# A linear-attention and MLP kernel: the last chunk's attention with keys by halves of a block, and the last two stores on another queue

## The chip, the core and the metric

The kernel runs on one core of a Trainium2 chip. The core has five engines that run side by side, each through its own list of instructions: TensorE (PE in the profile; its weight loads are listed apart as PEld), VectorE (DVE), ScalarE (ACT), GpSimd (POOL) and SyncE (SP). An instruction waits until the semaphores that it names have reached their values, and everything behind it on its engine waits with it. SP, ACT and POOL can also start DMA transfers; the profile calls the issuing lists SPq, ACTq and POOLq.

The metric is the device time of one execution in microseconds (us). The kernel before took 207.64 us as the median of three runs (207.38 to 207.97).

## The reference

Inputs are q, k, v of shape (4, 8, 768, 64) in fp32 (batch, heads, tokens, head size), one decay `lam` per head, and the two matrices and the slopes of an MLP. Attention is causal and decays with distance; it is computed in blocks with a running state. Its output, laid out as 3072 tokens by 512 features, goes through the MLP.

```python
intra = np.einsum('bhic,bhjc->bhij', qb, kb) * Dmask[None]      # Dmask = lam**(i-j) where i >= j, else 0
intra = np.einsum('bhij,bhjd->bhid', intra, vb)
inter = np.einsum('bhid,bhde->bhie', qb * lam_pow[None], kv_state)
out[:, :, sl] = intra + inter
kv_state = lam_block * kv_state + np.einsum('bhsd,bhse->bhde', kb * rev_pow[None], vb)
...
h = x @ w_in
g = np.maximum(h, 0.0) + alpha * np.minimum(h, 0.0)
return g @ w_out
```

The reference uses blocks of 64 tokens; the kernel uses blocks of `L` = 128, which is the same sum cut in another place.

## The kernel before, in words

**Chunks and units.** The 3072 tokens are cut in six chunks `c` = 0 to 5 (`NC` = 6) of 512 tokens: two of the four sequences times a window of 256 tokens (two blocks of 128, called a = 0 and 1 below). A chunk's attention is four *units* (`units`, numbered 0 to 23): one sequence and four of its heads each. Units 20 to 23 are the last chunk, `c` = 5.

**Layout.** Loads put tokens 2p and 2p+1 on partition p, so that a partition holds an even and an odd token (`e` = 0, 1). Each run that a load of k, q or raw v copies is 128 fp32 numbers, 512 bytes. `load` starts loads of k and q on SP (some early ones on POOL), `load_v16` starts those of v on POOL, one per unit, which cast to fp16 on the way; a unit's v is a tile of its own, from eight buffers.

**One unit.** `casts` turns k and q to fp16 (on ACT, for units 19 on) and multiplies k by its decay on POOL (`key_decayed`, L291, tile `kdec`). `transposes` (called through `turned`) has SP start a DMA transpose that gives `qkT`. `decayed` (L355, POOL) multiplies the transposed q by its decay, giving `qdT`. Then `cluster(old, new)` puts these on PE in a row: `inter(old)` (L375), `score_products(new)` (L391), `intra(old)` (L416), `state_products(new)` (L436). `score_products` and `intra` are 16 matmuls each: 64 by 64 corners of the array, four of them (the list `QUADS`) side by side in the array, each streaming 128 query columns. Half of the 128 keys of a block (the even or the odd ones) meet all its 128 queries in one matmul. `masked` (L402, DVE) multiplies the 1024 score columns by the decay mask (tile `dmask`, one fp32 value per score), which also sets the scores above the diagonal to zero. `attended` (ACT, L250) takes the sum to the tile `xT`, and `states` updates the running state on DVE (L465, tile `R`).

**The MLP.** `up` (L545) computes 128 rows of h on PE into a PSUM tile `h_ps`; ACT takes the negative part (L553, tile `m`), DVE finishes g (L560). `down` (L573), and for chunks 3 to 5 `down2` and `down2_last` (L655), multiply g by the second matrix. The latter use a scheme of seven instead of eight half products: sums of the halves of w_out are made on DVE (`weight_sum`, L621, tile `w_sum`) and sums of the halves of g on POOL and DVE (`g_sum`, L638).

**Order.** The order is written by hand and is the program order on every engine. Chunks 0 to 2 are a long list of calls. From chunk 3 on, a loop over `order[c]` alternates `up` of chunk c and `down` of chunk c-1 (each 0.86 us of PE), and the table `plan[c]` names what is called in front of the x-th of them. In chunk 3 the loop calls the loads of k and q for units 20 to 23 (x = 0 and 13), the preparation of units 19 to 23, and `cluster(16, 17)` to `cluster(19, 20)`; in chunk 4 `cluster(20, 21)` to `cluster(23, None)`. Chunk 5 has the MLP alone, and behind it stands `down2_last(5)`.

**The end.** `down2_last` finishes one output tile after the other. The last is computed as two times 128 columns (tile `p4`, written `p` in the profile): eight matmuls, an add on DVE (L719), a store by `write`, twice. All stores are started by SP. After them SP waits for the transfers that are still under way, and the engines meet at a barrier.

**DMA semaphores.** SP's transfers take eight semaphores in turn. A transfer waits, at its issue, until the one eight places before it has landed.

Of the kernel before, what the change touches and what calls it, by code (L numbers as in the profile page):

```python
# [11 lines left out]
def kernel(  # L12
# [33 lines left out]
    CH = 2 * W  # L46

# [3 lines left out]
    kv_pool = ctx.enter_context(tc.tile_pool(name="kvh", bufs=8))  # L51
    qkt_pool = ctx.enter_context(tc.tile_pool(name="qkt", bufs=3))
# [27 lines left out]
    def load(c, bi, x, half=None, queue="S"):  # L80
# [7 lines left out]
        i = "kqv".index(x)  # L88
        (nc.gpsimd if queue == "G" else nc.sync).dma_start(
# [130 lines left out]

    llp = const.tile([128, NHP], fp32, name="llp")
# [41 lines left out]
    def cast(n, name, eng):  # L263
        t = T.setdefault(n, {})
        if name == "v16":
            t[name] = kv_pool.tile([128, 4, 2, D], fp16, tag=name, name=name)
# [6 lines left out]

    def load_v16(n):

        c, bi, hh = units[n]
        v16 = kv_pool.tile([128, 4, 2, D], fp16, tag="v16", name="v16")
# [9 lines left out]
    def key_decayed(n, eng="G"):  # L287
        hh = units[n][2]
        kr = raw_of(n)["k16"]
        kdec = kv_pool.tile([128, 2, 4, D], fp16, tag="kdec", name="kdec")  # L290
# [3 lines left out]
            in1=kdecay[:, ds(4 * hh, 4), :].rearrange("p h e -> p e h").unsqueeze(3).to_broadcast([128, 2, 4, D]),  # L294
# [104 lines left out]
    def masked(n):  # L399
        t = T[n]  # L400
        t["sm"] = sm_pool.tile([128, 2, 2, 2, L], fp16, tag="sm", name="sm")
        nc.vector.tensor_tensor(  # L402
# [6 lines left out]
    def intra(n):  # L409
        t = T[n]  # L410
        pb = units[n][0] // 2
        for hp in range(2):
            for e in range(2):
                for hl, a in QUADS:
                    p = ds(a * 64, 64)
                    nc.tensor.matmul(  # L416
                        ot[a][ds(hl * 64, 64), hp, :],
                        lhsT=t["v16"][p, 2 * hp + hl, e, :],
                        rhs=t["sm"][p, hl, hp, 1 - e, :],
# [244 lines left out]
    def write(c, e, half, o, b=None, of=ds(0, 256)):  # L664
# [3 lines left out]
        if b is None:  # L668
            nc.sync.dma_start(out=to, in_=o)
        else:  # L670
            nc.sync.dma_start(out=to[:, b, of], in_=o)
# [34 lines left out]
    def down2_last(c):  # L706
# [3 lines left out]
        for i, side, b in order:  # L710
# [3 lines left out]
            if (i, b) == (4, 1):  # L714
                for x, bank in enumerate(("s", "acc")):
# [4 lines left out]
                    write(c, 1, 0, o, b, ds(128 * x, 128))  # L720
# [208 lines left out]
    query_decay(3, 0)  # L929
    up(1, 2, None, "h")  # L930
# [39 lines left out]
    down(1, 3, 0, 4, "op")  # L970
    down(1, 0, 2, 4, "tk")
# [67 lines left out]
    def prepared(n):  # L1039
        casts(n, "AA")  # L1040

    def turned(n):
        transposes(n, "D", False)
# [9 lines left out]
            13: lambda: (turned(20), decayed(19), load(5, 1, "k"), load(5, 1, "q")),  # L1053
            17: lambda: prepared(21),
            18: lambda: cluster(18, 19),
            20: lambda: (turned(21), decayed(20)),
            24: lambda: prepared(22),
# [78 lines left out]
```

## Time and profile before

| what | value |
|---|---|
| median of three runs | 207.64 us |
| the profiled execution's own time | 207.89 us |
| its span, first to last instruction | 206.1 us |
| PE busy | 200.1 us, 97% of the span |
| DVE, ACT, POOL busy | 77%, 55%, 54% |
| granted PE clock | 0.996 of full |
| the stage from 104 to 134 us | chunk 3's loop: `up` of chunk 3, `down` of chunk 2, units 16 to 20 |
| the stage from 134 to 162 us | chunk 4's loop as far as unit 23 |
| the stage from 162 us on | the MLP alone |

In the profile a group's row gives source line, engine, operation, tiles and shapes, the count, then busy time in us and the mean time of one in ns, then how long the engine stood idle in front of these and what it waited for. In a timeline, rows begin with the start and the length of a merged run of instructions, in us. Matmuls overlap, so the distance between starts is what one costs when the engine is full, not its own length.

### The profile page before, as it was taken

Reading aid. Unit: us, or ns where it says so; the run is one execution under the profiler, and the core shown is the slowest. Engines: PE = TensorE matmul, PEld = TensorE weight load, DVE = VectorE, ACT = ScalarE, POOL = GpSimd, SP = SyncE. Lnnn points to the kernel's source line nnn. Section 1 sums busy time; section 2 is a strip of 40 time slices with the busy share of each in tenths; the row PEclk is TensorE's granted clock in tenths of the full one; section 3 lists DMA queues with packets and bytes.
Section 4 is the critical chain, followed back from the end, with each engine's and each line's share of the span. In section 5 each row is a group of like instructions: output and inputs, shape, how many; then the busy total and the mean of one; then the engine's idle time right before and its main releaser. Section 6 shows DMA issues by size and latency. Waiting matters only on the chain.

```text
span 206.1 us, 5587 instructions
## 1 busy us (share of the span) xinstructions
PE 200.1 (97%) x2271; PEld 122.8 (60%) x2271; DVE 159.1 (77%) x289; ACT 113.6 (55%) x210; POOL 110.3 (54%) x132
## 2 busy tenths in 40 slices
PE   7999999999999999999999999999999999999991
PEld 6976445556445465555555455467667666667881
DVE  6978889568889647899998897959999466675921
ACT  7885778144776218656767466643543644444220
POOL 8999794043468893196356995562094040642000
PEclk9999999999999999999999999999999999999998
DMA  6999999997999998999969974441001201012222
GB/s 164 277 197 234 244 260 206 234 287 231 225 230 257 203 237 189 245 158 125 188 108 276 213 176 88 64 102 42 12 0 54 90 15 51 2 54 71 83 77 79
DMA packets 58206, 31.18 MB, mean 151 GB/s; under 512 B 27124, under 2 KB 55940, under 8 KB 58180
## 3 DMA queue, kind: packets, MB, share of 16 engines
q1 hardware_dynamic: 43028, 21.25, 42.5%
q0 software_dynamic: 15136, 9.57, 29.3%
q8 instruction: 18, 0.29, 0.6%
q14 instruction: 8, 0.07, 0.1%
q10 hardware_dynamic: 16, 0.00, 0.0%
HBM read 27.27 MB, written 6.29 MB: 163 GB/s over the span
## 4 chain that ended last, share of the span: by engine, by line
PE 92%; DVE 2%; ACT 2%; issue 1%; ACTq 0%; DVEq 0%
PE h_ps L545 39%; PE o_ps L573 21%; PE o_ps L655 16%; PE s L391 4%; PE acc L416 3%; PE unread L152 3%; PE acc L375 2%; PE tpx L341 2%; PE acc L436 1%; DVE g L638 1%; ACT L180 1%; ACT m L553 1%; ACT xT L250 1%; DVE sm L402 1%; PE p L655 0%
## 5 line engine op out<-in xcount | busy, mean ns | idle before, releaser
L545 PE MATMUL h_ps<-xT,w_in_sb 128*128 128x512 f16 (+1 forms) x392 | 91.9, 375 | 0.2 <-DVE g L560 0.2
L560 DVE SCALAR_TENSOR_TENSOR g<-m,oma,h_ps 128x512 f16<-128x512 f32 (+1 forms) x98 | 71.1, 734 | 24.9 <-ACT m L553 21.7
L553 ACT ACTIVATE m<-h_ps 128x512 f32<-128x512 f32 (+1 forms) x98 | 57.3, 588 | 46.3 <-PE h_ps L545 40.3
L545 PEld LDWEIGHTS <-w_in_sb 128*128 128x128 f16 x392 | 37.6, 98 | 37.4 <-issue 0.4
L573 PE MATMUL o_ps<-w_out_sb,g 128*128 128x512 f16 x192 | 46.8, 380 | 0.0
L402 DVE TENSOR_TENSOR sm<-s,dmask 128x1024 f16<-128x1024 f32 x24 | 29.2, 1219 | 11.7 <-PE s L391 11.7
L655 PEld LDWEIGHTS <-g 128*128 128x128 f16 x296 | 28.2, 98 | 8.2
L638 POOL TENSOR_TENSOR s<-g 128x512 f16<-128x512 f16 x11 | 13.0, 1179 | 32.8 <-PE o_ps L655 16.7
L573 PEld LDWEIGHTS <-g 128*128 128x128 f16 x192 | 17.7, 98 | 19.4 <-DVE g L560 0.2
L250 ACT ACTIVATE xT<-acc 128x512 f16<-128x512 f32 x24 | 14.3, 597 | 24.2 <-PE acc L436 22.2
L355 POOL TENSOR_TENSOR qdT<-qkT,qdecay 128x512 f16<-128x512 f16 (+1 forms) x19 | 20.5, 1082 | 7.6 <-DMA qkT<-qk 4.5
L655 PE MATMUL o_ps<-w_out_sb,g 128*128 128x256 f16 x192 | 24.1, 273 | 0.0
L291 POOL TENSOR_TENSOR kdec<-kraw,kdecay 128x512 f16<-128x512 f32 x18 | 20.0, 1116 | 6.1 <-DMA kraw<-in_k_dram 6.0
L254 POOL CAST qk<-qraw 128x512 f16<-128x512 f32 x12 | 7.6, 637 | 16.7 <-DMA qraw<-in_q_dram 15.9
L465 DVE SCALAR_TENSOR_TENSOR R<-R,rdecay,acc 128x128 f16<-128x128 f16 x54 | 15.5, 340 | 0.0
L278 POOL DMA_DIRECT2D v<-in_v_dram x19 | 14.9, 789 | 0.4 <-issue 0.4
L638 POOL TENSOR_TENSOR g<-g 128x512 f16<-128x512 f16 x11 | 13.3, 1207 | 0.9
L687 ACT ACTIVATE o_sb<-o_ps 128x512 f32<-128x512 f32 (+1 forms) x15 | 7.5, 497 | 7.6 <-PE o_ps L655 7.6
L655 PE MATMUL o_ps<-w_sum,g 128*128 128x256 f16 x88 | 11.3, 273 | 0.0
L391 PE MATMUL s<-qkT 64*64 64x128 f16 x384 | 10.1, 221 | 0.0
L416 PE MATMUL acc<-sm,v 64*64 64x128 f16 x384 | 9.8, 218 | 0.0
L690 DVE TENSOR_TENSOR o_sb<-o_sb,o_ps 128x512 f32<-128x512 f32 (+1 forms) x12 | 6.5, 549 | 4.2 <-PE o_ps L655 2.2
(84 smaller groups left out, 194.2 us busy)
## 6 DMA issues: line engine op xcount, KB each, us to landing
out_dram<-o_sb SPq DMA_DIRECT2D x20, 256.0 KB, 3.0
kraw<-in_k_dram SPq DMA_DIRECT2D x7, 512.0 KB, 5.3
qraw<-in_q_dram SPq DMA_DIRECT2D x6, 512.0 KB, 5.5
v<-in_v_dram POOLq DMA_DIRECT2D x19, 128.0 KB, 5.1
w_in_sb<-in_moe_w_in_dram POOLq DMA_DIRECT2D x4, 512.0 KB, 8.5
w_out_sb<-in_moe_w_out_dram POOLq DMA_DIRECT2D x4, 512.0 KB, 10.5
qraw<-in_q_dram POOLq DMA_DIRECT2D x6, 256.0 KB, 7.1
qraw<-in_q_dram SPq DMA_DIRECT2D x6, 256.0 KB, 4.8
```

Source lines behind the costliest of these rows:

```text
L250: nc.scalar.activation(out, in_, AF.Copy)
L291: engine(eng).tensor_tensor(out=kdec, in0=kr, in1=kdecay[:, ds(4 * hh, 4), :].rearrange("p h e -> p e h").unsqueeze(3).to_broadcast([128, ...
L355: engine(eng).tensor_tensor(out=qdT[:, :, :, p], in0=(t["qps"] if eng == "P" else t["qkT"][:, 0])[:, :, :, p], in1=qdecay[:, hh, :, :, p], ...
L391: nc.tensor.matmul(t["s"][ds(a * 64, 64), hl, hp, 1 - e, :].rearrange("p (e j) -> p e j", e=2), lhsT=t["qkT"][p, 1, e, hp, ds(a * 64, 64)] ...
L402: nc.vector.tensor_tensor(out=t["sm"].rearrange("p a h x j -> p (a h) x j"), in0=t["s"].rearrange("p a h x j -> p (a h) x j"), in1=mask_of ...
L416: nc.tensor.matmul(ot[a][ds(hl * 64, 64), hp, :], lhsT=t["v16"][p, 2 * hp + hl, e, :], rhs=t["sm"][p, hl, hp, 1 - e, :], start=(2 * pb + a ...
L545: nc.tensor.matmul(h_ps[:, 0:n] if bi is None else h_ps[:, 0:n].rearrange("p (e j) -> p e j", e=2), lhsT=w_in_sb[:, gi, ts(f, 128)], rhs=x ...
L553: nc.scalar.activation(m[:, 0:n], h_ps[:, 0:n], AF.Relu, scale=-1.0)
L560: nc.vector.scalar_tensor_tensor(out=g, in0=mv, scalar=oma[:, f : f + 1], in1=hv, op0=ALU.mult, op1=ALU.add)
L573: nc.tensor.matmul(o_ps, lhsT=lhs(c, f, t), rhs=w_out_sb[:, f, :], start=(f == 0), stop=(f == NF - 1),)
L638: engine(eng).tensor_tensor(out=out, in0=in0, in1=in1, op=op)
L655: nc.tensor.matmul(t[:, cols], lhsT=x, rhs=w, start=(fresh and f == 0), stop=(last and f == NF // 2 - 1), skip_group_check=True,)
```

## The change

**Keys by halves, for the last chunk alone.** For units 20 to 23 the two groups of keys on a partition are no longer even and odd tokens but the first 64 and the last 64 tokens of the block (`f` = 0, 1 in place of `e`). The queries stay in even and odd order. Keys of the second half are above the diagonal for the first 64 queries, so their matmuls stream 64 columns in place of 128, in `score_products` and in `intra`: 192 of 256 columns. `masked` multiplies 768 columns in place of 1024, with a mask `HM` in the new order.

**What the new order needs.** k of this chunk is loaded by four DMAs per sequence in place of one, in runs of 64 numbers. v is loaded by `load_vh`, four DMAs per sequence (for two units) in place of two. The key decay is computed a second time for the new order (`half_positions` on POOL, `half_key_decay` on ACT, both in earlier chunks' code). The new masks are put together from `dmask`: `half_mask` starts four DMAs on SP from SBUF to SBUF per group of heads, `later_half` copies the columns of the second half on POOL.

**v tiles for two units.** v tiles now hold the eight heads of a sequence, from four buffers, in all chunks.

**The last two stores** are started by ACT in place of SP.

```diff
+    HC = NC - 1
...
+        if x == "k" and c >= HC:
+            for a in range(2):
+                for f in range(2):
+                    nc.sync.dma_start(
+                        out=raws[c, bi][x][ds(64 * a, 64), heads, ds(D * f, D)],
+                        in_=k[b, heads, ds(pb * W + L * a + 64 * f, 64), :].rearrange("h p d -> p h d"),
+                    )
+            return
...
+    def half_positions():
+        for half in range(2):
+            nc.gpsimd.iota(
+                rev_i[ds(half * 64, 64)], pattern=[[-64, 2]], base=L - 1, channel_multiplier=-1
+            )
+        nc.gpsimd.tensor_copy(out=rev_h, in_=rev_i)
+
+    def half_key_decay():
+        for f in range(2):
+            nc.scalar.activation(hdecay[:, :, f], loglam, AF.Exp, scale=rev_h[:, f : f + 1])
...
+    def half_mask(hh):
+        m = [dmask[:, x].rearrange("p l h a j -> p (l h) (a j)") for x in range(2)]
...
+        for a in range(2):
+            for e in range(2):
+                nc.sync.dma_start(
+                    out=HM[hh][64 * a + e : 64 * a + 64 : 2, :, 0:L],
+                    in_=m[hh][ds(64 * a, 32), :, ds(64 * (1 - e), L)],
+                )
+
+    def later_half(hh):
+        nc.gpsimd.tensor_copy(
+            out=HM[hh][:, :, L:192].rearrange("p x (e j) -> p x e j", e=2),
+            in_=HM[hh][:, :, 0:L].rearrange("p x (e j) -> p x e j", e=2)[:, :, :, 0:32],
+        )
...
+    def load_vh(bi, a):
...
+        for f in range(2):
+            nc.gpsimd.dma_start(
+                out=V[HC, bi][ds(64 * a, 64), :, f],
+                in_=v[2 * (HC % 2) + bi, :, ds((HC // 2) * W + L * a + 64 * f, 64), :].rearrange("h p d -> p h d"),
+            )
...
+        if units[n][0] >= HC:
+            s = t["s"].rearrange("p l h x j -> p l h (x j)")
+            for hp in range(2):
+                for f in range(2):
+                    for a, hl in QUADS:
+                        p = ds(hl * 64, 64)
+                        nc.tensor.matmul(
+                            s[ds(a * 64, 64), hl, hp, ds(L * f, L - 64 * f)].rearrange("p (e j) -> p e j", e=2),
+                            lhsT=t["qkT"][p, 1, f, hp, ds(a * 64, 64)],
+                            rhs=t["qkT"][p, 0, :, hp, ds(a * 64 + 32 * f, 64 - 32 * f)],
+                            start=True,
+                            stop=True,
+                        )
+            return
...
+        if units[n][0] >= HC:
+            out, in0 = (y.rearrange("p a h x j -> p (a h) (x j)")[:, :, 0:192] for y in (t["sm"], t["s"]))
+            nc.vector.tensor_tensor(out=out, in0=in0, in1=HM[units[n][2]], op=ALU.mult)
+            return
...
-            nc.sync.dma_start(out=to[:, b, of], in_=o)
+            queue.dma_start(out=to[:, b, of], in_=o)
...
-                    write(c, 1, 0, o, b, ds(128 * x, 128))
+                    write(c, 1, 0, o, b, ds(128 * x, 128), nc.scalar)
...
         3: {
...
+            3: lambda: half_mask(0),
...
-            10: lambda: prepared(20),
+            10: lambda: (load_vh(0, 0), prepared(20)),
...
+            22: lambda: later_half(0),
```

The remaining entries of the table stand in the same loop; the following rows of the program's order show where they come out.

**SP in chunk 3**, from the loads of the last chunk's first sequence to those of its second (`kraw`, `qraw`: raw k and q; `qkT`: a transpose; `out_dram`: a store of chunk 2). Before:

```order
L89 DMA kraw<-in_k_dram 128x8x128
L89 DMA qraw<-in_q_dram 128x8x128
L311 DMA_TRANSPOSE qkT<-qk_2245 128x8x128
L589 DMA out_dram<-o_sb 128x512
L311 DMA_TRANSPOSE qkT<-qk_2360 128x8x128
L89 DMA kraw<-in_k_dram 128x8x128
L89 DMA qraw<-in_q_dram 128x8x128
L589 DMA out_dram<-o_sb 128x512
```

Now, over the same stretch of SP (`hmask` and `dmask` as targets are the new masks):

```order
L94 DMA kraw<-in_k_dram 64x8x64 x4
L99 DMA qraw<-in_q_dram 128x8x128
L257 DMA hmask<-dmask 32x4x128 x4
L378 DMA_TRANSPOSE qkT<-qk_2248 128x8x128
L679 DMA out_dram<-o_sb 128x512
L378 DMA_TRANSPOSE qkT<-qk_2371 128x8x128
L94 DMA kraw<-in_k_dram 64x8x64 x4
L99 DMA qraw<-in_q_dram 128x8x128
L257 DMA dmask<-dmask 32x4x128 x4
L679 DMA out_dram<-o_sb 128x512
```

In front of the transpose of unit 19 (the first of the two) stand nine transfers where there were two, and in front of the second store nine where there were two.

**POOL in the same chunk**, from the v load of unit 20 on (`s`, `g`: the sums of halves of g, L638). Before:

```order
L278 DMA v_2363<-in_v_dram 128x4x128
L291 TENSOR_TENSOR kdec<-kraw,kdecay 128x512
L355 TENSOR_TENSOR qdT<-qkT,qdecay 128x512
L278 DMA v_2478<-in_v_dram 128x4x128
L291 TENSOR_TENSOR kdec<-kraw,kdecay 128x512
L638 TENSOR_TENSOR s_2221<-g_2237 128x512
L638 TENSOR_TENSOR g_2237<-g_2237 128x2x256
L355 TENSOR_TENSOR qdT<-qkT,qdecay 128x512
L638 TENSOR_TENSOR s_2221<-g_2353 128x512
```

Now:

```order
L335 DMA v_2368<-in_v_dram 64x8x64 x2
L358 TENSOR_TENSOR kdec<-kraw,hdecay 128x512
L422 TENSOR_TENSOR qdT<-qkT,qdecay 128x512
L335 DMA v_2368<-in_v_dram 64x8x64 x2
L358 TENSOR_TENSOR kdec<-kraw,hdecay 128x512
L728 TENSOR_TENSOR s_2221<-g_2240 128x512
L728 TENSOR_TENSOR g_2240<-g_2240 128x2x256
L422 TENSOR_TENSOR qdT<-qkT,qdecay 128x512
L264 COPY hmask<-hmask 128x4x64
L728 TENSOR_TENSOR s_2221<-g_2361 128x512
```

Each v load has become two, and a copy for the mask stands in front of the second pair of sums; the second sequence repeats this.

**The end of ACT**. Before, ACT's list ended with its evacuations, and SP's with seven stores of 256 columns and two of 128:

```order
L687 ACTIVATE o_sb<-o_ps 128x256 x6
L685 ACTIVATE o_sb<-o_ps 128x256
L687 ACTIVATE o_sb<-o_ps 128x256
L1131 UNCONDITIONAL_BRANCH
```

Now the two stores of 128 columns stand at the end of ACT's list:

```order
L777 ACTIVATE o_sb<-o_ps 128x256 x6
L775 ACTIVATE o_sb<-o_ps 128x256
L777 ACTIVATE o_sb<-o_ps 128x256
L761 DMA out_dram<-o_sb 128x128 x2
L1226 UNCONDITIONAL_BRANCH
```

PE's list has the same instructions in the same order; 32 score matmuls and 32 of `intra` are half as wide.

More of the change, by code (lines that the diff above doesn't have):

```diff
@@ L289, in key_decayed @@
         kr = raw_of(n)["k16"]
+        decay = hdecay if units[n][0] >= HC else kdecay
         kdec = kv_pool.tile([128, 2, 4, D], fp16, tag="kdec", name="kdec")
@@ L293, in key_decayed @@
             in0=kr,
-            in1=kdecay[:, ds(4 * hh, 4), :].rearrange("p h e -> p e h").unsqueeze(3).to_broadcast([128, 2, 4, D]),
+            in1=decay[:, ds(4 * hh, 4), :].rearrange("p h e -> p e h").unsqueeze(3).to_broadcast([128, 2, 4, D]),
             op=ALU.mult,
@@ L662, in product, with write @@
             )
-    def write(c, e, half, o, b=None, of=ds(0, 256)):
+    def write(c, e, half, o, b=None, of=ds(0, 256), queue=nc.sync):
         pb = c // 2
```

39 lines of the change are left out of this document (32 added, 7 removed).

## The prediction, made before the changed kernel had run

> **What bounds the kernel now.** I read the busy time by stage first, for the span that the change touches:
>
> ```profile
> core 0: us, PE busy (x) PEld busy (x) DVE busy (x) ACT busy (x) POOL busy (x), PEclk, DMA share, GB/s
> 104.00:134.00 30.00, 30.00 (x298) 15.26 (x297) 26.49 (x40) 18.55 (x33) 21.00 (x20) 1.00 0.79 159
> 134.00:147.00 13.00, 12.79 (x130) 8.89 (x127) 10.09 (x18) 6.02 (x11) 4.59 (x4) 1.00 0.23 62
> 162.00:201.00 39.00, 39.00 (x295) 28.45 (x293) 24.17 (x48) 16.61 (x31) 9.33 (x8) 1.00 0.15 52
> ```
>
> PE is busy without a gap, at full clock, save for 0.21 us between 134 and 147. So a column less on PE is time gained, and a wait that reaches PE is time lost at its full length. The waits from 103 to 146 name that gap, and the chain shows what follows PE at the end:
>
> ```profile
> PE h_ps L545 <- DVE g L560: 0.2, 1, 0.2
> ...
> 201.00 0.91 PE p L655 x16
> 201.90 0.02 issue
> 201.93 0.29 DVE o_sb L719
> ```
>
> The last add ends at 202.22, the span at 206.1: 3.9 us of stores and barrier, in which no engine computes. The change touches three places: PE's columns, DVE's gap, this tail.
>
> **Part 1: PE's columns.** How many matmuls of four corners side by side cost is read from the growth of a merged run, four matmuls at a time. 128 columns (L416) and 64 columns (L436), both in the cluster of units 8 and 9:
>
> ```profile
> 65.42 0.23 PE L416 MATMUL acc<-sm,v 64*64 64x128 f16 x4
> 65.42 0.39 PE L416 MATMUL acc<-sm,v 64*64 64x128 f16 x16
> ...
> 65.64 0.20 PE L436 MATMUL acc<-v,kdec 64*64 64x64 f16 x4
> 65.64 0.29 PE L436 MATMUL acc<-v,kdec 64*64 64x64 f16 x16
> ```
>
> Twelve more matmuls, three groups, take 0.16 us with 128 columns (0.053 a group) and 0.09 with 64 (0.030). A unit has four groups in the scores and four in `intra`, and half of them shrink: 4 x 0.023 = 0.09 us, for four units 0.37 us. If groups went by columns alone it would be 0.43; if they did not shrink, 0. The weight loads are as many as before and already keep up with 0.030. I take 0.37.
>
> **Part 2: DVE's mask and the gap.** Where the gap ends, DVE has worked without a pause:
>
> ```profile
> 140.15 0.75 DVE L560 SCALAR_TENSOR_TENSOR g<-m,oma,h_ps 128x512 f16<-128x512 f32 x1 [0.32 <-ACT m L553]
> 140.82 1.29 DVE L638 TENSOR_TENSOR g<-s,g 128x512 f16<-128x512 f16 x1
> 142.63 1.21 DVE L402 TENSOR_TENSOR sm<-s,dmask 128x1024 f16<-128x1024 f32 x1
> 144.28 0.73 DVE L560 SCALAR_TENSOR_TENSOR g<-m,oma,h_ps 128x512 f16<-128x512 f32 x1
> 145.06 1.02 PE L545 MATMUL h_ps<-xT,w_in_sb 128*128 128x512 f16 x4 [0.21 <-DVE g L560]
> 140.66 1.16 POOL L355 TENSOR_TENSOR qdT<-qkT,qdecay 128x512 f16<-128x512 f16 x1 [3.11 <-PE acc L375]
> ```
>
> The mask of unit 21 stands in that row of DVE work. With 768 of 1024 columns, 1.21 us becomes 0.91 if it goes by columns; nothing is gained if it is all fixed cost, which a mask of 1024 columns hardly is. I take 0.25 of the 0.30, more than the gap, so 0.21 us is gained. The other three masks are beside a busy PE and gain nothing. Late next on DVE would be the same g (L560) of the following `up`, which has no wait today.
>
> **Part 3: the tail.** SP's last three stores and what lies around them:
>
> ```profile
> 201.48 1.18 SPq L671 DMA_DIRECT2D out_dram<-o_sb  x1
> 202.75 0.38 SPq L671 DMA_DIRECT2D out_dram<-o_sb  x1
> 203.23 0.41 SPq L671 DMA_DIRECT2D out_dram<-o_sb  x1
> ...
> 201.54 0.68 DVE L719 TENSOR_TENSOR o_sb<-o_sb,p 128x128 f32<-128x128 f32 x2
> ...
> DMA to landing us min/median/max: 1.7/1.9/2.7
> out_dram<-o_sb SPq DMA_DIRECT2D x2, 64.0 KB, 1.7
> out_dram<-o_sb SPq DMA_DIRECT2D x1, 128.0 KB, 2.7
> q8 instruction: 1, 0.02, 100.9%
> 0.73 0.59 ACTq L62 DMA_DIRECT2D lam_sb<-in_lam_dram  x1
> ```
>
> The store ahead (128 KB) holds SP for 1.18 us where others take 0.38; the row of queue q8, from 200.6 to 200.7, shows a fetch of instructions that occupies a whole DMA engine just then, so I take the store to wait for that engine. The two small stores then start at 202.75 and 203.23, though their adds ended at 201.8 and 202.2. The last lands at 203.23 + 1.7 = 204.9. On ACT, idle there, they start at about 201.87 and 202.26 with an issue of 0.38, or 202.46 with the 0.59 of ACT's one DMA, and land by 204.0 to 204.2. SP's 128 KB store lands at 201.48 + 2.7 = 204.2 and is then the last. Gain: 204.95 - 204.2 = 0.75 us. Ends: if that store were quicker too (1.9 to landing), 0.95; if ACT were held as SP is (1.18 for the first), the second would start at 203.05 and land at 204.75, gain 0.2. No row makes it a loss: even the longest plain store's issue leaves ACT ahead of SP.
>
> The Trainium skill (DMA: Bandwidth & Descriptors, "Issuing engines are not separate DMA queues") says that transfers started by several engines run on the same DMA engines and that only the issuing time is saved, usually a small one. By that rule with the usual 0.38 us the tail would gain 0.4 and the sum be 206.7; the trace's row of 1.18 us is not small, and I go by the row.
>
> **Part 4: what is added, and its cover.** SP issues 14 transfers more. In front of the transpose of unit 19 stand nine where two stood:
>
> ```profile
> 104.74 0.57 SPq L89 DMA_DIRECT2D kraw<-in_k_dram  x1
> 106.18 3.31 SPq L311 DMA_TRANSPOSE qkT<-qk  x1
> ...
> kraw<-in_k_dram SPq DMA_DIRECT2D x1, 512.0 KB, 5.3
> qkT<-qk SPq DMA_TRANSPOSE x1, 3.2
> ...
> 119.44 0.42 PE L391 MATMUL s<-qkT 64*64 64x128 f16 x16
> ```
>
> Through the eight semaphores the transpose also waits for the second of the four k loads: issued at about 105.2 and landing 5.3 later, at 110.5. Transposed 3.2 us after that, unit 19 is there at 113.7; PE needs it at 119.4. Behind SP's queue stand a store (its buffer comes round two stores later) and the transposes of units 20 and 21, which PE needs in its later clusters. I cost it at nothing; without that cover each us on SP would be one on PE. The q load of unit 20 lands later by the issues ahead of it, and ACT, which casts it, has later `m` behind it; ACT is busy 18.55 us of this stage's 30 and DVE 26.49, so a delay under a us is caught up before it reaches PE: I take 0 and keep 0.5 us of loss as the end.
>
> POOL gets four v loads and two copies more in the stage:
>
> ```profile
> 109.21 0.79 POOL L278 DMA_DIRECT2D v<-in_v_dram  x1
> 126.12 1.27 POOL L638 TENSOR_TENSOR s<-g 128x512 f16<-128x512 f16 x1 [2.63 <-DVE g L560]
> 134.04 1.15 POOL L638 TENSOR_TENSOR s<-g 128x512 f16<-128x512 f16 x1 [2.48 <-DVE g L560]
> L254 POOL CAST qk<-qraw 128x512 f16<-128x512 f32 x12 | 7.6, 637 | 16.7 <-DMA qraw<-in_q_dram 15.9
> ```
>
> 4 x 0.79 = 3.2 us, and the copies, half as wide as the casts, 2 x 0.35: 3.9 us. The two idle times shown hold 5.1. So POOL is late in between, but about on time at 140.66. The ends are 0 and the price of the third case below; I take 0. The new decay is two activations of ACT and three small instructions of POOL:
>
> ```profile
> L219 ACT ACTIVATE kdecay<-loglam,rev_f x2: 286/286/287, 4.9 to 5.1; 128x8 f32<-128x8 f32 x2
> ...
> 73.95 0.60 ACT L250 ACTIVATE xT<-acc 128x512 f16<-128x512 f32 x1 [4.69 <-PE acc L436]
> ```
>
> 0.57 us in a part of ACT that idles for 4.69 us, and on POOL under 0.9 beside a full PE: nothing. v tiles for two units come round after the same eight units: nothing.
>
> **Sum.** 0.37 + 0.21 + 0.75 = 1.33 us off the profiled execution's 207.89 (span 206.1, 1.8 around it) gives 206.56. That execution is 0.25 above the median of 207.64, so the median becomes 206.3.
>
> **The rivals.** *The tail gains little:* ACT is held by the same DMA engine as SP. For it, 1.18 us on SP; against it, ACT's own list of transfers is empty there. Gain 0.37 + 0.21 + 0.2: 206.9.
>
> *DVE is pushed by a late POOL.* DVE's sums of two SBUF tiles take 0.42 or 1.40 us, the longer while POOL works:
>
> ```profile
> 118.03 1.40 DVE L621 TENSOR_TENSOR w_sum<-w_out_sb,w_sum 128x512 f16<-128x512 f16 x1
> 125.95 0.42 DVE L621 TENSOR_TENSOR w_sum<-w_out_sb,w_sum 128x512 f16<-128x512 f16 x1
> ```
>
> If POOL's sums shift by over 3 us into 137 to 142, the DVE sums there lose a us in all, the gap grows by 0.65 instead of closing, and late weight sums cost up to 0.5 more near 127: 207.64 - 0.37 - 0.75 + 0.65 + 0.5 = 207.7, no change. The Trainium skill (SBUF — State Buffer, "Who interferes with whom") says that a DVE instruction with two SBUF inputs and a POOL instruction that reads SBUF exclude each other for a whole instruction. The trace agrees with 1.40 against 0.42.
>
> *Slower: SP is held.* If most of the nine transfers hold SP as the 1.18 and 3.31 us rows do, unit 19 comes too late. The transpose must start by 119.4 - 3.2 = 116.2, which leaves 11.5 us, 1.27 each. At 1.6 us each it starts at 119.1, PE waits 2.9 us, and with 1.33 gained: 209.2. Against it: the short rows, 0.38 to 0.57, are the rule.
>
> *The matmuls don't shrink:* the 0.030 us groups speak against it; it would cost 0.37 and give 206.7, inside the forecast.
>
> **How the numbers follow.** The forecast 206.3 has a chance of 0.56; small tail 0.14; late POOL 0.16; held SP 0.14. The lower end is 0.43 + 0.21 + 0.95 and 0.2 of scatter below 207.64, 205.8; the upper end takes in the late POOL, 207.9; left out is the held SP. The forecast's own range is 205.9 to 206.8. About 0.3%, 0.62 us, is what a measurement can tell here: faster is below 207.0, the first two cases less a little, 0.68; the same is the third and edges, 0.17; slower 0.15.
>
> **What would show it.** Score groups of 64 columns 0.03 us apart; masks of about 0.95 us; no wait of `h_ps` for g near 145; two ACTq stores at 201.3 and 201.7 (all is 0.6 earlier) and the last landing about 1.3 earlier than today. Against it: PE idle at unit 19's scores, ACT waiting at unit 20's q cast, or DVE sums of 1.2 us between 137 and 142.

## The result, and the profile after

The changed kernel takes 207.69 us (median; 207.26 to 208.08), the kernel before measured beside it 207.70 (207.38 to 208.57). The ratio is 0.9997, with an interval of 0.9986 to 1.0009: no difference. Measured again later it was 207.23 (206.66 to 208.78) against 207.63, ratio 0.9989 (0.9966 to 1.0012). The forecast was 206.3.

The profiled execution took 208.08, with a span of 206.3. The stages of it, with the columns of the prediction's first view:

```profile
104.00:134.00 30.00, 29.14 (x292) 14.65 (x291) 24.38 (x38) 17.54 (x32) 21.43 (x23) 1.00 1.09 172
134.00:147.00 13.00, 12.96 (x126) 8.61 (x125) 11.20 (x20) 6.30 (x12) 6.26 (x7) 1.00 0.40 72
```

The idle time has moved. PE, full from 104 to 134 before, now stands still there for 0.86 us, while the gap between 134 and 147 has gone from 0.21 to 0.04. PE's waits, with the rows of PE, DVE and ACT that lead to them:

```profile
PE h_ps L635 <- DVE g L650: 0.9, 2, 0.4
...
116.12 1.02 PE L635 MATMUL h_ps<-xT,w_in_sb 128*128 128x512 f16 x4 [0.44 <-DVE g L650]
118.43 0.81 PE L635 MATMUL h_ps<-xT,w_in_sb 128*128 128x512 f16 x3 [0.42 <-DVE g L650]
...
115.32 0.75 DVE L650 SCALAR_TENSOR_TENSOR g<-m,oma,h_ps 128x512 f16<-128x512 f32 x1 [3.57 <-ACT m L643]
...
111.58 0.63 ACT L298 ACTIVATE qk<-kraw 128x512 f16<-128x512 f32 x1 [0.61 <-DMA kraw<-in_k_dram]
114.17 0.63 ACT L298 ACTIVATE qk<-qraw 128x512 f16<-128x512 f32 x1 [1.96 <-DMA qraw<-in_q_dram]
114.71 0.58 ACT L643 ACTIVATE m<-h_ps 128x512 f32<-128x512 f32 x1
```

Read from the bottom. ACT's two casts of unit 20 wait for their loads, 0.61 us for k and 1.96 for q. The `m` queued behind them starts at 114.71, g follows at 115.32 after DVE had nothing to do for 3.57 us, and PE, which needs that g before it can go on with `up`, waits twice. The two rows show 0.86 us of idle time and the starts of the matmuls step back by 0.61 and 0.58 there: a matmul's row lasts 0.38 us, while the next one starts after 0.22, so a row's end hides a part of the delay. In the kernel before neither cast waited for its load. Its row of the q cast stands first, then SP's issues of before and of after:

```profile
111.58 0.63 ACT L250 ACTIVATE qk<-qraw 128x512 f16<-128x512 f32 x1
112.26 0.60 ACT L553 ACTIVATE m<-h_ps 128x512 f32<-128x512 f32 x1
...
105.36 0.64 SPq L89 DMA_DIRECT2D qraw<-in_q_dram  x1
```

```profile
104.59 3.36 SPq L94 DMA_DIRECT2D kraw<-in_k_dram  x4
107.99 0.63 SPq L99 DMA_DIRECT2D qraw<-in_q_dram  x1
108.67 0.66 SPq L257 DMA_DIRECT2D hmask<-dmask  x1
...
qraw<-in_q_dram SPq DMA_DIRECT2D x1, 512.0 KB, 6.2
hmask<-dmask SPq DMA_DIRECT2D x4, 64.0 KB, 5.6
v<-in_v_dram POOLq DMA_DIRECT2D x2, 64.0 KB, 5.7
```

The four k parts hold SP for 3.36 us, so q is issued 2.63 us later than before, and it lands 6.2 us after that, at 114.15. One of the four stands out: the second, issued at 105.40, takes 1.19 us where the others take 0.63 to 0.76. Beside it the trace has a fetch of instructions, one packet of 16 KB from 105.28 to 106.16.

To see where time comes and goes along the whole program, the starts of PE's matmuls can be set against those of the kernel before, number by number, since both have 2271. The columns below are the difference in us (negative: earlier than before) at matmul 1000 (77 us, what the start has given), 1500 (118 us), 1800 (147 us) and at the last.

```
                       1000    1500    1800    last
changed kernel        -0.15   +1.03   +0.67   +0.44
loss, 1000 to 1500           +1.18
columns and gap, 1500 to last         -0.59
```

The start differs by tenths from trace to trace, in kernels with the same code there as well (-0.45 to +0.34 in all the traces that follow), and is set apart for that reason. The loss of 1.18 us is the two waits. After it the change brings what it was to bring: 0.59 us, of which the step at the former gap is 0.17 and eight steps of 0.05, one for each of the four units' scores and one for each `intra`, are 0.40. That gap, in DVE's and PE's rows:

```profile
141.80 1.29 DVE L728 TENSOR_TENSOR g<-s,g 128x512 f16<-128x512 f16 x1
143.02 0.67 DVE L780 TENSOR_TENSOR o_sb<-o_sb,o_ps 128x512 f32<-128x512 f32 x1
143.61 0.94 DVE L485 TENSOR_TENSOR sm<-s,dmask 128x768 f16<-128x768 f32 x1
145.00 0.73 DVE L650 SCALAR_TENSOR_TENSOR g<-m,oma,h_ps 128x512 f16<-128x512 f32 x1
...
145.78 0.59 PE L635 MATMUL h_ps<-xT,w_in_sb 128*128 128x512 f16 x2
```

The mask takes 0.94 us instead of 1.21, and the matmul at 145.78 waits for no g. The tail of the changed kernel (PE, the stores' issues, their time to landing, POOL's steps in the end barrier), and POOL's steps in the kernel before. In POOL's rows, the numbers behind the colon are the shortest, median and longest duration in ns, then the first and the last start in us:

```profile
201.27 1.06 PE L745 MATMUL p<-w_sum,g 128*128 128x128 f16 x16
202.29 0.85 ACTq L761 DMA_DIRECT2D out_dram<-o_sb  x2
...
201.92 1.01 SPq L761 DMA_DIRECT2D out_dram<-o_sb  x1
...
out_dram<-o_sb ACTq DMA_DIRECT2D x2, 64.0 KB, 2.0
...
L1226 POOLq DRAIN  x2: 51/76/102, 205.4 to 206.0; - x2
L1226 POOLq EVENT_SEMAPHORE_RANGE_CLEAR  x1: 139/139/139, 205.9 to 205.9; - x1
```

```profile
L1131 POOLq DRAIN  x2: 51/76/102, 205.5 to 205.8; - x2
L1131 POOLq EVENT_SEMAPHORE_RANGE_CLEAR  x1: 139/139/139, 205.7 to 205.7; - x1
```

From the start of the last matmul to the last landing it is 2.60 us instead of 3.27, a gain of 0.67. From there to the end it is 1.61 instead of 1.18, a loss of 0.43, because POOL pauses in the barrier: its first drain ends at 205.52 and the clear of semaphores starts at 205.86, where before these were 0.03 apart. So the tail gained 0.25. The whole: -0.15 (start) + 1.18 (loads) - 0.59 (columns, gap) - 0.25 (tail) = +0.19, the difference of the spans.

Three theories went into the experiments. A: unit 20's k and q land too late, and this alone hides gains that are real. B: the gains are not real. C: POOL, later by its added loads and copies, is what delays g.

### The profile page after: what moved, and what is told of

The parts are those of the page before. It is cut to its first block, busy times and chain, and to the rows that moved or that the text cites. A ratio compares the mean times of both kernels' runs of the same rounds, so it can differ in the third digit from the quotient of the medians.

```text
span 206.3 us, 5624 instructions
## 1 busy us (share of the span) xinstructions
PE 200.0 (97%) x2271; PEld 122.6 (59%) x2271; DVE 158.5 (77%) x289; ACT 113.9 (55%) x212; POOL 113.3 (55%) x141
## 4 chain that ended last, share of the span: by engine, by line
PE 76%; issue 5%; POOL 5%; DMA 5%; SPq 3%; ACT 2%; DVE 1%; ACTq 0%; POOLq 0%
PE h_ps L635 31%; PE o_ps L745 17%; PE o_ps L663 15%; DMA qraw<-in_q_dram 5%; PE unread L162 3%; PE s L472 2%; PE acc L506 2%; POOL qdT L422 2%; PE tpx L408 2%; PE acc L442 2%; SPq L94 2%; POOL kdec L358 1%; POOL v L344 1%; SPq L378 1%; PE acc L526 1%
## 5 line engine op out<-in xcount | busy, mean ns | idle before, releaser
L487 DVE TENSOR_TENSOR sm<-s,dmask 128x1024 f16<-128x1024 f32 x20 | 24.4, 1219 | 11.3 <-PE s L472 11.3
L422 POOL TENSOR_TENSOR qdT<-qkT,qdecay 128x512 f16<-128x512 f16 (+1 forms) x19 | 21.1, 1114 | 10.4 <-DMA qkT<-qk 7.9
L358 POOL TENSOR_TENSOR kdec<-kraw,kdecay 128x512 f16<-128x512 f32 x14 | 14.7, 1054 | 5.9 <-DMA kraw<-in_k_dram 5.9
L344 POOL DMA_DIRECT2D v<-in_v_dram x15 | 11.7, 783 | 0.4 <-issue 0.4
L302 POOL CAST qk<-kraw 128x512 f16<-128x512 f32 x9 | 5.5, 614 | 8.2 <-DMA kraw<-in_k_dram 8.2
L506 PE MATMUL acc<-sm,v 64*64 64x128 f16 (+1 forms) x384 | 9.4, 216 | 0.0
```

Source lines behind the costliest of these rows:

```text
L344: nc.gpsimd.dma_start(out=v16.rearrange("p h e d -> p h (e d)"), in_=v[2 * (c % 2) + bi, ds(4 * hh, 4), ds((c // 2) * W, W), :].rearrange( ...
L358: engine(eng).tensor_tensor(out=kdec, in0=kr, in1=decay[:, ds(4 * hh, 4), :].rearrange("p h e -> p e h").unsqueeze(3).to_broadcast([128, 2 ...
L422: engine(eng).tensor_tensor(out=qdT[:, :, :, p], in0=(t["qps"] if eng == "P" else t["qkT"][:, 0])[:, :, :, p], in1=qdecay[:, hh, :, :, p], ...
L487: nc.vector.tensor_tensor(out=t["sm"].rearrange("p a h x j -> p (a h) x j"), in0=t["s"].rearrange("p a h x j -> p (a h) x j"), in1=mask_of ...
```

## The experiments

**The loads of unit 20 first.**

```diff
-            0: lambda: (turned(18), load(5, 0, "k"), load(5, 0, "q"), decayed(17)),
+            0: lambda: (load(5, 0, "k"), load(5, 0, "q"), turned(18), decayed(17)),
```

> The changed kernel with one step moved: the four k loads and the q load of unit 20 are issued ahead of the transpose of unit 18 instead of behind it, so about 5 us earlier. Theory A (the loss is unit 20's k and q landing late: ACT's two casts wait 0.61 and 1.96 us, m and g come later by it, PE stands still for 0.44 + 0.42 us in `up`): the casts find their data, both waits of h_ps for g go, and the time is about 1.15 us below the changed kernel, 206.5. Rival B (the gains on PE's columns and in the tail are not there, and the waits near 116 are caught up by PE later): 207.4 to 207.9. Rival C (POOL, later by its four loads and two copies, holds DVE's g): the waits of h_ps stay near 116 and the time stays within 0.3 us of 207.7. If the transpose of unit 18 becomes late by the five issues ahead of it (about 3 us), PE waits at unit 18's scores instead: up to 208.5.

Measured: 206.96 us (206.83 to 207.02), ratio to the kernel before 0.9967 (0.9955 to 0.9979). ACT's two casts and PE's stage:

```profile
110.71 0.62 ACT L298 ACTIVATE qk<-kraw 128x512 f16<-128x512 f32 x1
111.23 0.62 ACT L298 ACTIVATE qk<-qraw 128x512 f16<-128x512 f32 x1
...
104.00:134.00 30.00, 30.00 (x299) 15.31 (x298) 26.08 (x40) 18.30 (x34) 23.17 (x26) 1.00 0.99 156
```

Neither cast waits, PE is full from 104 to 134, and between matmuls 1000 and 1500 nothing is lost; from 1500 to the last 0.60 us is gained. B and C fall: with POOL's added work unchanged the waits are gone, and the columns' and the gap's gain is there. The median is 0.73 below the changed kernel's and not 1.15, which the next runs bear on.

**Only k in four parts**, in the kernel before.

```diff
+        if x == "k" and c >= NC - 1:
+            for a in range(2):
+                for f in range(2):
+                    nc.sync.dma_start(
+                        out=raws[c, bi][x][ds(64 * a, 64), heads, ds(D * f, D)],
+                        in_=k[b, heads, ds(pb * W + L * a, L), :].rearrange("h (p e) d -> e p h d", e=2)[f],
+                    )
+            return
```

> The kernel before, with nothing changed but that the last chunk's k is loaded by four transfers of 256-byte runs in place of one of 512-byte runs, into the same layout. Theory A: the four issues and the slower landing put unit 20's q cast behind by 1 to 2.5 us as in the changed kernel, PE waits about 0.9 to 1.15 us near 116, and the time is 208.6 to 208.9. If only the issues ahead of the load count and not the runs (in the changed kernel the k loads were also issued behind nothing else), less: 207.9 to 208.3. Rival B and rival C: the loads are hidden, 207.5 to 207.9.

Measured: 208.2 us (208.1 to 208.56), ratio 1.0034 (1.0021 to 1.0046). ACT's rows:

```profile
111.36 0.63 ACT L258 ACTIVATE qk<-kraw 128x512 f16<-128x512 f32 x1 [0.27 <-DMA kraw<-in_k_dram]
113.13 0.63 ACT L258 ACTIVATE qk<-qraw 128x512 f16<-128x512 f32 x1 [1.14 <-DMA qraw<-in_q_dram]
```

The casts wait 1.41 us together, and PE does not feel it: the matmuls stand within 0.03 us of the kernel before from number 1000 to the last. So the slack behind these casts is 1.41 us or more, and k in four parts uses 1.41 of it. The time of 208.2 agrees with one of the expected figures and not with its reason: the spans of its runs have a median of 206.1 against 205.9, and what lies outside the span is 2.11 us against 1.77 in the kernel before. What these 0.34 us are stays open; the changed kernel, with the same split, has 1.79.

**What is issued behind q.** The hmask copies were moved behind the transpose of unit 19; then, in a second kernel, the v loads beside q as well.

```diff
-            3: lambda: half_mask(0),
...
+            9: lambda: half_mask(0),
```

```diff
-            10: lambda: (load_vh(0, 0), prepared(20)),
+            10: lambda: (reserve(20), reserve(21), prepared(20)),
...
-            17: lambda: (load_vh(0, 1), prepared(21)),
+            17: lambda: (load_vh(0, 0), load_vh(0, 1), prepared(21)),
```

`reserve` only assigns the tile of v. 

> The changed kernel with one step moved: the four copies that fill hmask of units 20 and 22 are issued behind the transpose of unit 19 and the store after it, 3 us later than now, so that nothing of SP's stands between q's issue and that transpose. k in four parts stays where it was. In the run with only k in four parts q of unit 20 landed at 113.1 and no wait of PE followed; in the changed kernel, with the hmask copies and two v loads beside it, at 114.15, and PE lost 1.15 us. Theory A2 (k's parts use up the slack, and what is issued right behind q, sharing the DMA engines with it, makes the loss): q lands near 113.2, the waits of h_ps for g near 116 go or fall below 0.2 us, 206.6 to 206.9. Theory A1 (the late issue of k and q is enough by itself): q lands as late as before, PE keeps 0.9 to 1.15 us, 207.5 to 207.8. If the v loads, which POOL issues, are what slows q: half of it stays, 207.1 to 207.3.

> The kernel with the hmask copies behind the transpose of unit 19, and now also the two v loads of POOL that stood beside q (at 109.3 and 110.0 us) put 7 us later, to the next two. What is left in front of unit 20's q are the four parts of k. With hmask alone moved, q landed at 113.6 in the profiled run and the median was 207.17, half of the loss back. Theory A2 (the traffic beside q makes the loss, hmask and v a half each): q lands at 113.1 as with k in four parts alone, PE waits under 0.1 us near 116, 206.6 to 206.8. Theory A1 (the four parts of k make the other half): no change from 207.17. If the v loads come too late for the units that need them, PE waits near 137: above 207.5.

Measured: 207.17 us (206.79 to 207.91), ratio 0.9974 (0.9958 to 0.999), and 207.29 (206.56 to 207.91), ratio 0.9986 (0.9974 to 0.9997). ACT's rows, hmask moved and then both moved:

```profile
111.31 0.63 ACT L298 ACTIVATE qk<-kraw 128x512 f16<-128x512 f32 x1 [0.32 <-DMA kraw<-in_k_dram]
113.61 0.63 ACT L298 ACTIVATE qk<-qraw 128x512 f16<-128x512 f32 x1 [1.67 <-DMA qraw<-in_q_dram]
```

```profile
111.11 0.63 ACT L298 ACTIVATE qk<-kraw 128x512 f16<-128x512 f32 x1 [0.31 <-DMA kraw<-in_k_dram]
113.12 0.63 ACT L298 ACTIVATE qk<-qraw 128x512 f16<-128x512 f32 x1 [1.38 <-DMA qraw<-in_q_dram]
```

PE lost 0.61 and 0.31 us between matmuls 1000 and 1500. Each step took some of the traffic away that stands beside q, and q's time from issue to landing fell from 6.2 us to 5.3 and 5.2. That is theory A2's order, but its under 0.1 us of waiting and its 206.6 to 206.8 for the second kernel were missed; a median that does not move is what A1 expected there. The next run shows 5.45 us with all the traffic in place, so these traces do not show that the traffic makes the difference. In the first of the two PE also lost 0.41 us at 132.3, which the first trace of the changed kernel does not have. What released PE there is a g of DVE, late behind a mask and a weight sum (L711) of 1.76 us. That fits a part of the prediction's rival of the late POOL, the late weight sums near 127.

**The changed kernel once more**, unaltered.

> The changed kernel once more, unaltered, for a second trace of it. Its profiled execution (span 206.3) was the longest of its twelve runs (205.5 to 206.3), and in it PE lost 1.18 us near 116, while the kernel with the loads ahead, which loses nothing there, is only 0.73 us shorter in the medians. In five traces the loss is what ACT's two casts of unit 20 wait beyond 1.41 us: 0.27 + 1.14 gave 0, 0.31 + 1.38 gave 0.31, 0.32 + 1.67 gave 0.61, 0.61 + 1.96 gave 1.18. Theory A: the same relation holds here, whatever q's landing is; if the span is near the median of 205.85, the loss is 0.5 to 0.9. If the loss is 1.2 again in a run of ordinary length, the medians' difference is made elsewhere, at the start or in the tail.

Measured: 207.23 us, runs from 206.66 to 208.78. The profiled execution is one of the short ones, 206.66 with a span of 204.9:

```profile
110.57 0.62 ACT L298 ACTIVATE qk<-kraw 128x512 f16<-128x512 f32 x1
112.71 0.63 ACT L298 ACTIVATE qk<-qraw 128x512 f16<-128x512 f32 x1 [1.51 <-DMA qraw<-in_q_dram]
...
104.00:134.00 30.00, 30.00 (x300) 15.31 (x298) 25.38 (x40) 18.16 (x33) 23.66 (x26) 1.00 1.05 172
```

The same program lost nothing here. Its four k parts held SP for 2.89 us instead of 3.36 and q landed 5.45 us after its issue instead of 6.16. The shorter hold goes with the 16 KB fetch: here it starts at 105.19, just behind the second k part, which was issued at 105.10 and takes 0.62 us. In the five other traces with this order of loads the fetch starts 0.05 to 0.12 us ahead of the second part, which takes 1.19 to 1.43. Set side by side, with the same kernels and one more (the changed kernel with the last stores back on SP), the wait of the two casts in us and PE's loss between matmuls 1000 and 1500:

```
                                   casts wait   PE loses
only k in four parts                  1.41        0.01
changed kernel, second trace          1.51        0.01
hmask and v later                     1.69        0.31
hmask later                           1.99        0.61
stores back on SP                     2.55        1.16
changed kernel, first trace           2.57        1.18
loads ahead                           0           0
```

Above 1.4 us each further us of wait is, within 0.1 us, a us of PE. The changed kernel stands at the edge of this slack, and how far over it falls differs from execution to execution with the issue and the landing of q. So the first trace, of the longest of twelve runs, can show more loss (1.18) than the medians: the kernel's first median is 0.73 above the one with the loads ahead, its second 0.27. The price of the late loads is thus 0.3 to 0.7 us; two traces of the kernel do not fix it better.

**The stores**, put on ACT in the kernel before, and taken back in the changed kernel.

```diff
-                    write(c, 1, 0, o, b, ds(128 * x, 128))
+                    write(c, 1, 0, o, b, ds(128 * x, 128), nc.scalar)
```

> The kernel before, with the last two stores on ACT's queue and nothing else. The forecast's own step: 0.75 us faster, 206.9. The changed kernel's trace, where the last landing came 0.68 us closer to PE's end but the barrier behind it took 0.4 us longer: 0.25 to 0.3 us faster, 207.4. Rival B (the tail gains nothing): 207.7. If the longer barrier belongs to the changed program's length and not to the stores, 0.6 to 0.7 us faster, 207.0.

> The changed kernel with the last two stores back on SP's queue. Forecast's step: 0.75 us slower than the changed kernel, 208.4. The trace of the changed kernel: 0.25 to 0.3 us slower, 208.0. Rival B: 207.7. The two runs with the stores, put on or taken back, should give the same amount if the barrier's extra time goes with the stores; if it goes with the program, this one gives 0.6 to 0.7.

Measured: 207.21 us (207.08 to 207.46) with the stores moved alone, ratio 0.998 (0.9972 to 0.9989); 207.94 (207.2 to 209.06) with them taken back, 0.25 above the changed kernel. In the first, the end barrier takes 1.17 us behind the last landing as before; in the second 1.58, as in the changed kernel. So the 0.4 us of longer barrier go with the changed program, wherever the stores are. The times alone would not say so: of the stores put on, 0.46 us is between the two figures expected, and of the stores taken back, 0.25 is under the 0.6 to 0.7 (it is 0.71 against the changed kernel's second median). In the traces the time from the last matmul's start to the last landing is 2.56 with the stores moved alone, against 3.27, and 3.13 with them taken back, against 2.60.

**POOL's pause in the barrier.** Sixteen clears of one column, unused, were added to POOL's stream in the kernel with only the stores moved.

```diff
+    for _ in range(16):
+        nc.gpsimd.memset(filler, 0.0)
```

> The kernel with only the stores moved, and 16 clears of one column, that nothing uses, put into POOL's stream near 73 us, where POOL idles. In the changed kernel and its two variants POOL, which has 200 records instead of 184, pauses 0.33 us between its last two steps of the end barrier (0.03 in the kernel before and its two variants). Theory L (the pause goes with the length of POOL's stream): the pause is there, the time behind the last landing grows from 1.17 to 1.55 us, 207.5 to 207.6. Theory M (it goes with the kind of instructions or with the DMA queues that the changed kernel uses): no pause, 207.2.

Measured: 208.37 us (207.32 to 208.9). The barrier takes 1.61 us behind the last landing. POOL's rows in it:

```profile
L1134 POOLq DRAIN  x2: 93/146/198, 205.2 to 205.8; - x2
L1134 POOLq EVENT_SEMAPHORE_RANGE_CLEAR  x1: 142/142/142, 205.3 to 205.3; - x1
```

The pause is there, now behind the clear (which ends at 205.45, the second drain starts at 205.78): one step later, in a stream of 199 records against 200. It goes with the length of POOL's stream. The time rose by more: in this trace PE also waits for 0.4 us near 74, where the clears stand, and the rest, some 0.3 us, is not accounted for.

**The fetch in the tail.** The kernel with the loads ahead, less 24 of PE's idle matmuls at the start, which compute nothing.

```diff
-    tick(56, "tk")
+    tick(32, "tk")
```

> The kernel with the loads ahead, with 24 of the 56 idle matmuls at the start left out, which keep PE's clock up and compute nothing. PE's stream becomes shorter by those instructions, so that its last fetch of 16 KB, which lay at 199.8 us there and took 1.49 us, comes elsewhere or not at all. Theory F (SP's 128 KB store is held 1.0 to 1.2 us by that fetch): its issue takes under 0.6 us, it lands 0.5 us earlier or more, and with the two stores on ACT the last landing comes 0.2 to 0.5 us earlier: 206.5 to 206.8 if the start is as long as it was. If the store is held by something else (the store ahead of it, for instance): 1.0 to 1.2 us as before, and 206.9 to 207.0.

Measured: 206.32 us (206.31 to 206.56), ratio 0.9937 (0.9918 to 0.9956). SP's store, and the issues with their time to landing:

```profile
200.71 0.33 SPq L761 DMA_DIRECT2D out_dram<-o_sb  x1
...
out_dram<-o_sb SPq DMA_DIRECT2D x5, 128.0 KB, 1.9
out_dram<-o_sb ACTq DMA_DIRECT2D x2, 64.0 KB, 1.7
```

In its trace no fetch of PE's falls in the tail, the store takes 0.33 us to issue where it took 1.0 to 1.2, and the last landing comes 2.31 us after the last matmul's start instead of 2.71. Theory F holds: with the 16 KB fetch the store is held, without it not, and what lands beside it lands sooner. But of the 0.64 us between the medians the trace places 0.40 in the tail, and PE loses 0.25 near 131 to a late g as above. The same step from the kernel with only the stores moved (207.21) to the one below without the change (206.57) is worth 0.64 again, with 0.21 in the tail of their traces and 0.30 ahead of matmul 1000. So not all of it is shown to be the fetch.

**The pause moved**, with eight clears more on POOL, between two of its last sums.

```diff
-        5: {},
+        5: {12: lambda: [nc.gpsimd.memset(filler, 0.0) for _ in range(8)]},
```

> The kernel with the loads ahead and without the late fetch (206.32), and eight clears of one column, used by nothing, in POOL's stream between two of its last sums, where it idles. Theory L (POOL pauses where its stream comes to the end of what was fetched; 16 clears more in the kernel before made the pause appear, one step of the barrier later with one record less): eight more move the pause ahead of the barrier, where POOL waits anyway, so the time behind the last landing falls from 1.57 to about 1.17 us: 205.9. Theory M (the pause belongs to the barrier of this program): it stays, 206.3.

Measured: 206.1 us (206.01 to 206.56), ratio 0.9935 (0.9921 to 0.9949), the fastest kernel here. The barrier's rows:

```profile
L1227 POOLq DRAIN  x2: 51/76/102, 203.7 to 204.0; - x2
L1227 POOLq EVENT_SEMAPHORE_RANGE_CLEAR  x1: 139/139/139, 203.9 to 203.9; - x1
```

The pause is gone; the barrier takes 1.30 us behind the last landing instead of 1.57. So eight instructions more make this end 0.27 us shorter, less than the 0.4 expected. The medians are 0.22 apart, but the two ratios' intervals nearly coincide, so the times by themselves do not show a gain.

**The same surroundings without the change**: the kernel before, with the stores on ACT and 24 idle matmuls fewer.

> The kernel before, with the stores on ACT and 24 of the 56 idle matmuls at the start left out: what stands around the change in the fastest kernel so far (206.1), without the change's half blocks, loads, masks and v tiles. Theory A (half blocks are worth 0.37 us of PE's columns and 0.21 us of the gap once their loads come in time): PE's end differs from the fastest kernel's by 0.6 us, give or take 0.3 for the start, the store of 128 KB is issued in 0.33 us and 206.7 comes out. Rival B (the columns bring nothing on the chip, and the gains came from the stores and the fetch): 206.1 to 206.3.

Measured: 206.57 us (206.54 to 206.87), ratio 0.9948 (0.9932 to 0.9963). Its stages still have the old gap:

```profile
104.00:115.00 11.00, 11.00 (x131) 5.86 (x130) 7.33 (x13) 6.57 (x13) 5.94 (x7) 1.00 1.06 190
120.00:147.00 27.00, 26.79 (x239) 15.69 (x233) 24.54 (x40) 14.51 (x25) 15.15 (x14) 1.00 0.47 86
```

Against it the fastest kernel's PE gains 0.58 us from matmul 1500 on and gives back 0.12 in the barrier, together 0.46, next to the 0.47 us between the medians. (The two traces' spans differ by 0.77, since 0.26 lie ahead of matmul 1000 and 0.05 in the landing.) The two ratios' intervals overlap, so the times by themselves do not prove it; the traces place it.

**v tiles for two units alone**, in the kernel before.

```diff
-        v16 = kv_pool.tile([128, 4, 2, D], fp16, tag="v16", name="v16")
+        v16 = v_of(n)
```

> The kernel before, with the v tiles taken for two units at a time and nothing else. The forecast put this at nothing: 207.5 to 207.8. If a later release of a shared v tile holds back POOL's loads of v, and by that a unit: 208 or more.

Measured: 207.77 us (207.2 to 208.05), ratio 1.0002 (0.999 to 1.0014): nothing, as expected.

## Why the prediction was wrong, step by step

- **Part 1, PE's columns, right.** Forecast 0.37 us; between matmul 1500 and the last 0.58 to 0.60 us was gained in the traces where nothing else disturbed it, 0.17 of it at the gap, and 0.04 at an `up` near 154. The columns are the eight steps of 0.05, 0.40, between the forecast and the end that goes by columns alone (0.43).
- **Part 2, the mask and the gap, right.** 1.21 to 0.94 us, and 0.17 of the 0.21 us gap.
- **Part 3, the tail, right in its mechanism and too large.** Forecast 0.75 us (ends 0.2 and 0.95). ACT did start the stores at 202.29 and 202.71 without being held, and SP's store was the one held, by the fetch, as argued. (The row of q8 with 100.9% is of a stretch of 0.1 us; the fetch is one packet of 1.61 us.) But the stores landed 2.0 us after their issue and not 1.7, so the landing gained 0.67 in the trace, and the stores alone gained 0.46 in the medians. The Trainium skill's rule (DMA: Bandwidth & Descriptors, "Issuing engines are not separate DMA queues"), by which only the issuing time is saved, would have made it 0.4; the measured 0.46, with an interval of 0.23 to 0.58, is nearer to that. No step had the 0.4 us that the changed program loses in the barrier: the sum put that at nothing without naming it.
- **Part 4, the step that failed.** It reads: "The q load of unit 20 lands later by the issues ahead of it ... a delay under a us is caught up before it reaches PE: I take 0 and keep 0.5 us of loss as the end." That a delay of that size is caught up was true, with more room than stated: 1.4 us of ACT's waiting. The delay was mis-sized. By the q row of the same trace (105.36, 0.64 us), four issues of that length in place of one at 0.57 put q 2.0 us later; with SP held once, it was 2.6 in the first trace. Its landing took 5.0 us with k in four parts alone and 5.5 to 6.2 in the changed kernel; whether the hmask and v traffic makes that difference stays open. The price of this step was not 0 but, in the medians, the 0.3 to 0.7 us that issuing the loads earlier gave back, and 1.18 in the first profiled execution. The end of 0.5 us kept for it was too small for the first median and the first trace.
- **The rest of Part 4 held.** The transpose of unit 19 was issued only at 111.5, behind SP's other issues, and PE met unit 19's scores at 120.5 without a wait. POOL was late in 137 to 142: a pair of its sums starts at 135.66 instead of 134.04, and one of DVE's sums there takes 1.13 us instead of 0.49. No wait of PE came of it in the changed kernel's traces, and with the loads moved alone its waits are gone, so the late POOL does not explain the result. It is not free, however: in two variants a late weight sum cost PE 0.25 and 0.41 us near 131. The v tiles cost nothing in a run of their own; the added decays, at 60 and 74 us of the first trace, had none, but PE does not fall behind the kernel before there (-0.11 us at matmul 500, -0.15 at 1000).
- **The rivals.** The outcome, no change, was given to the late POOL with 0.16; the mechanism was the one that the prediction named as evidence against itself, ACT waiting at unit 20's q cast, and that had no chance of its own.

Put together: 0.6 of columns and gap and 0.46 of stores, less 0.4 of barrier and about 0.7 of late loads, leave nothing of the 1.33 us of the sum. Without the late loads 0.66 would be left, and the kernel with the loads ahead gained 0.71. Measured again, the changed kernel was 0.4 below the one before, within the noise; then the late loads cost 0.3.

## What to carry to other kernels

When a load is split, add up the issues on its queue one by one as far as the first engine that waits for the data, and compare the sum with the slack behind that engine; a stage's mean idle time does not show that slack. A program at the edge of its slack needs more than one trace: here one lost 1.18 us and the next one nothing. A load that nothing holds back belongs in front of a transpose that waits.

## What the runs showed of the hardware that was not expected

- **A fetch of instructions can hold a transfer's issue.** With a 16 KB fetch in the tail the store ahead took 1.0 to 1.2 us to issue, without it 0.33 (three traces), and the tail was 0.2 to 0.4 us shorter. The same fetches stand beside the k part that took 1.19 us. Not every issue is held: in the kernel before a store at 155.56 takes 0.38 us beside a fetch from 155.51 to 156.43. The Trainium skill (Advanced Engine Details and Errata, "ISA Cache") gives lines of 16 KB for 256 instructions. The trace agrees roughly: 18 fetches for PE's 4553 records, 253 to a fetch, and 17 for the 4505 that are left with 24 idle matmuls fewer, 265 to one. So the place of a fetch moves with the number of instructions ahead of it.
- **POOL's barrier has a pause of 0.3 us that depends on how long POOL's stream is:** with 184 and 188 records none, with 199 and 200 one, a step apart, and with eight instructions more than 200 none in the barrier. A fetch goes with it: each of the eight traces with the pause has one more fetch of 8 KB, 1.0 to 1.3 us after the pause begins, the five traces with 184 or 188 records have none there, and with eight instructions more one stands at 178 instead. That the pause is POOL's waiting for instructions is an inference from this; since the recorded fetch starts behind the pause, the link between them stays open.
- **Issues on SP that nothing holds come to 0.60 to 0.76 us each, one behind the other, whatever their size:** k parts of 128 KB, q of 512 KB and mask copies of 64 KB alike in the changed kernel, most of them 0.63, where its late stores of 128 KB take 0.33. The forecast had reckoned with 0.38 to 0.57.
